# Seven block products for four more MLP tiles ahead of the attention loop, and three queries made inside the loop

## Chip, cores and metric

One core of one Trainium2 chip runs the whole kernel. The metric is the device time of one execution in microseconds. Five engines work side by side: the matrix engine (PE, with its weight loads listed as PEld), the vector engine (DVE), the activation engine (ACT), the general engine (POOL) and the engine that issues most transfers (SP). Matrix results go to PSUM banks, which DVE and ACT read.

## What is computed

The reference normalises x, runs attention of 32 heads over cached keys and values and an MLP mixer on the same normalised rows, and joins both with a gate:

```python
xn = _layernorm(x)                                   # 2048 x 512
# attention: q = xn @ wq, 32 heads of 128
scores = einsum("bhqd,bhkd->bhqk", q, k_cache) * 128 ** -0.5
s = softmax(scores) @ v_cache  ->  heads joined  @ wo
# MLP: D = 512, F = 1792
h = gelu(layernorm(xn) @ w1); hs = shifted(h) @ w2; x1 = xn + hs
g = silu(x1 + gelu(layernorm(x1) @ w3) @ w4)
return x + s * g
```

Inputs and output are bf16.

## The kernel before

**Tiles.** The 2048 rows are 16 tiles of 128 rows, four tiles make a chunk `c` of 512 rows.

**The MLP comes first.** `m1`, `m2` and `x1` make the first half of the MLP; `m3(c, f)` makes, for chunk `c`, a seventh of the 1792 hidden columns as 8 matmuls of 512 columns into a buffer `ps_s` (two buffers), and ACT's gelu writes it to `h2[c]`. The last product with `w4` is made in one of two ways:

- `pair_out(t)` takes tiles t and t+1 together and forms their product from seven block products, each 7 matmuls of 256 columns (49 in all), instead of 28 matmuls of 512. The block sums of the hidden rows come from `h_sums(t)`, four DVE instructions on 128x896 elements (L931). The results are put together by DVE additions (L948) while the products run, out of the banks `psX` (`xa` or `xm`, one buffer each, for `pa`) and `ps_o` (two buffers, for `pb` and `pc`). A second product is accumulated into `pb` and into `pc` after the first was read.
- A *held* tile is made as 14 matmuls of 512 columns, `m4`, that `held_mm(n)` spreads over the slots of the attention loop; when a tile is done, `held_out` adds it to `xall` (DVE), and two and four slots later the tanh (ACT) and the gate (DVE) follow.

Before the change tiles 0 to 7 go by pairs and tiles 8 to 15 are held. `gate_pair(t)` makes the gates of two tiles that went by pairs.

**The attention loop.** A unit is one head and one chunk of 512 query rows; there are 128 units, numbered in groups of 4 heads by 4 chunks, each of 8 slots (slot number n = 8u + p). In slot n, PE makes two score matmuls into `ps_s` (`s_slot`), ACT takes the exponential of both (L446), and PE makes two matmuls with the values for slot n - 10 (`pv_run`). DVE adds the exponentials of a unit (`add_first`, `add_half`, `add_next`, `fold`, `fold_last`) and, a unit later, sums, inverts and applies the row sums. Half of one addition goes to POOL in the units of `APART`. Every engine takes its instructions in the order in which the program writes them.

**Queries.** `q_ahead(u)` makes the query of a unit during the MLP: 4 matmuls into bank `xa` or `xm`, by turns of the list `made`, and a copy by ACT. Units 0 to 7, then 8 to 10, then 127 are made in this way. Units that are not in `made` and lie before unit 14 get theirs in the loop, two units ahead: one matmul in each of slots 3 to 6 into `xa` and a copy by DVE in slot 7 (`q_copy`). From unit 14 on two heads' queries come from seven block products; their block sums are `x_sum` (L366, on the normalised rows) and `w_sum` (L375, on `wq`).

**Output projection.** `wo_todo` is a queue of tiles whose four heads are finished. One tile takes slots 3 to 7 (`wo_mm` into `xm`, then a DVE copy or addition in `wo_post`). The first four tiles have to wait until `sacc` can be placed, which is where the MLP's buffers were (the pool `pS`, opened once the held tiles are done). Most later ones are made with seven block products as well, with sums `wo_sum` (on `wo`) and `o_sum`, added up by `wo_take` (L596). `CATCH` lists slots of unit 8 in which the waiting tiles are made, `PLAN` overrides the slots of single units.

Of the kernel before, what the change touches and what calls it, by code (L numbers as in the profile page):

```python
# [11 lines left out]
BF16 = mybir.dt.bfloat16  # L12
# [5 lines left out]
def kernel(  # L18
# [16 lines left out]
    P = nc.NUM_PARTITIONS  # L35
# [3 lines left out]
    Sq, D = x2d.shape  # L39
    _, H, Sk, Dh = A_k_cache.shape  # L40
# [3 lines left out]
    NT = Sq // P  # L44
# [3 lines left out]
    FC = F // P  # L48
    EPS = 1e-5
    SCALE = float(Dh) ** -0.5  # L50
    HG = 4
    NG = H // HG

    SPU = KC // 2
# [34 lines left out]
    qtp = ent(pool("qt", 6))  # L89
# [11 lines left out]
    pR = right.enter_context(pool("pR", side="right", reuse_waits="tile"))  # L101
# [21 lines left out]
    HEAD = 7  # L123
    XS = 3 * QT + 1
    TW = (2, 1, 0, 1)
# [3 lines left out]
    NU = len(units)  # L129
# [201 lines left out]
               xnT[:, dc, qt * 512:(qt + 1) * 512], dc == 0, dc == DC - 1)  # L331

    def q_copy(u, eng=None):
        pl, tag = (pR, "qR") if u < HEAD else (qtp, "qT")
        qT = pl.tile([P, 512], BF16, tag=tag, **(dict(bufs=HEAD) if u < HEAD else {}), name="qT")
        src, dst = st[u].pop("psq")[:], qT[:]
        if u in TURN:
            src = src.rearrange("d (r j) -> d j r", j=4)
            dst = dst.rearrange("d (j r) -> d j r", j=4)
        if eng is None:  # L340
            pin(nc.vector.tensor_copy(out=dst, in_=src))
        else:
            pin(nc.scalar.activation(out=dst, in_=src, func=ACT.Identity))
        st[u]["qT"] = qT[:]
# [208 lines left out]
    def wo_sum(g, i):  # L553
        w = wog[g]
        b11, b12, b21, b22 = (w[:, k, c] for k in (UP, DOWN) for c in (WL, WR))
        if i == 2 and g < NG - 2:
            out = b12
        else:
            j = 0 if i == 2 else i
            out = pS.tile([P, 2, D // 2], BF16, tag=f"tw{j}", bufs=TW[j], name="tw")[:]  # L560
        a, b = ((b12, b11), (b22, tw.get((g, 0))), (b22, b12), (b21, tw.get((g, 1))))[i]
        pin(nc.vector.tensor_tensor(out=out, in0=a, in1=b, op=ALU.subtract))
        tw[g, i] = out
# [267 lines left out]
    def q_ahead(u):  # L831
        q_mm(u, range(DC), ("xa", "xm")[len(made) % 2])
        q_copy(u, nc.scalar)
        made.append(u)
# [33 lines left out]
        x1(t, ps)  # L868
    for t in range(4):
        stats(xall[:, t, :], mv2, rs2, t)  # L870
    for u in range(2 * HG, 2 * HG + 3):
        q_ahead(u)
    banks = [(psO, "ps_o")] * 2 + [(psX, "xa"), (psX, "xm")]
    for t in range(4, 8):
        if t == 7:
# [95 lines left out]
    def gate_pair(t):  # L971
        th = [gate_tanh(t + i) for i in range(2)]
        for i in range(2):
            gate_silu(t + i, th[i])

    for c in range(2):
        h_sums(4 * c)
        h_sums(4 * c + 2)
        pair_out(4 * c, lambda: None)
        pair_out(4 * c + 2, lambda: gate_pair(4 * c))  # L980
        for f in range(FC // 2):
            m3(2 + c, f)
            if f == 1:
                gate_pair(4 * c + 2)
    left.close()
    pB = left.enter_context(pool("pB", reuse_waits="tile"))

# [16 lines left out]
            at((b - 4 - hh // 2) * SPU + (5, 7)[hh % 2], lambda h=h: load_wo(h))  # L1004

    heldps = {}
    held = deque((t, fc) for t in range(8, NT) for fc in range(FC))

    def held_out(t, n):
        x2(t, heldps.pop(t))  # L1010
# [2 lines left out]
        at(n + 4, lambda: gate_silu(t, th["a"]))  # L1013

    def held_mm(n):
        for _ in range((4, 10)[n] if n < 2 else 3 if n < SPU + 2 else 2 if n < 2 * SPU else 1 + (n % SPU in (1, 5, 7))):
            if not held:
                return
            t, fc = held.popleft()
            if fc == 0:  # L1020
                heldps[t] = psX.tile([P, 512], FP32, tag=("xa", "xm")[t % 2], name="ps_m")
            m4(t, heldps[t], (fc,))
            if fc == FC - 1:
                held_out(t, n)
# [28 lines left out]

    FIRST, LAST = 14, NU - 4
    BLOCK = [(g, qt) for g in range(NG - 1) for qt in range(QT)][1:-2]
    APART = range(2 * HG + 1, NU - 3)
    pairs = range(FIRST, LAST + 1, 2)
    q_plan = defaultdict(list)
    steps = defaultdict(list)
# [21 lines left out]
            which[u0 + n].append((o_sum, g, qt, i))  # L1081
    for g in range(NG - 1):
        u0 = ((g * QT + (g == 0)) * HG + 6) * SPU
        for i, n in ((0, -4), (2, -4 if 0 < g < NG - 2 else 4), (1, 4), (3, 12)):
            o_early[u0 + n].append((wo_sum, g, i))
    for i, (qt, u) in enumerate((qt, qt * HG + 5 + j) for qt in range(1, QT) for j in range(2)):
        at(u * SPU + 6, lambda qt=qt, i=i: sa_clear(qt, i % 2))
# [3 lines left out]
    for i, u in enumerate((10, 11, 12, 13, 14, 16, 18, 20)):  # L1091
# [2 lines left out]
        at(n - 2 * SPU + 4, lambda t=t, i=i: gate_load(t, i))  # L1094
        at(n + 3, lambda t=t: y_scale(t))
        at(n + 6, lambda t=t: y_add(t))
    CATCH = {2 * HG * SPU + p: x for p, x in {
        0: ((0, "xa"),), 1: ((1, "xa"),), 2: ((2, "xa"),), 3: ((0, "xm"),), 4: ((1, "xm"),),
        5: ((2, "xm"), (0, "xa")), 6: ((1, "xa"),), 7: ((2, "xa"),)}.items()}
    PLAN = {2 * HG: (), LATER + 6: (), LATER + 7: ((2, 0), (3, 1), (7, 2)), LATER + 8: ((1, 0), (3, 1), (4, 2), (6, 0), (7, 1)),  # L1100
            LATER + 9: ((0, 2), (2, 0), (3, 1), (7, 2))}

    def add_last(u):
# [13 lines left out]
        for fn, *args in plan.get(n, ()):  # L1117
            fn(*args)

    for j, u in enumerate((9, 9, 9, 9, 12, 12, 13, 13, 13, 16, 17, 17, 18, 19, 20, 20)):  # L1120
        at(u * SPU + 3, lambda qt=(j // 4 - 1) % QT, i=j % 4: x_sum(qt, i))
    for h in range(2, H, 2):
        for i, u in enumerate((((-4, -3, -3, -3), (-1, -1, 0, 0))[h % HG // 2] if h >= HG else (11,) * 4)):
            o_early[(h // HG * QT * HG + u) * SPU + 4].append((w_sum, h, i))

    for v in range(1, NU):
# [4 lines left out]
    for n in range(UB * SPU):  # L1131
# [29 lines left out]
            fold_last(u - 1)  # L1161
        if p == 3 and u - 1 in TURN:
            turn(u - 1)
        for part, tag in CATCH.get(n, ()):
            wo_slot(part, n, tag=tag)
        for v, k in ((u + 1, 3), (u + 2, 7)):
            if p == k and "psq" in st.get(v, ()) and (k == 3) == (v > FIRST):
                q_copy(v)
# [200 lines left out]
```

## Time and profile before

| | |
|---|---|
| median of 3 runs | 1223.53 us (1222.01 to 1224.49) |
| the profiled execution | 1222.83 us, its span 1221.1 us |
| PE busy | 1208.6 us, 99% |
| ACT busy | 1107.6 us, 91% |
| DVE busy | 1089.9 us, 89% |
| POOL busy | 297.6 us, 24% |

The span runs from the first to the last instruction; the profiled time holds 1.7 us more around it. Durations of matmuls overlap: the engine starts the next one before the listed end of the last, so the rate is read from starts. A row of a timeline gives start, duration, engine, line, operation, tiles, forms and count, and in brackets how long the engine was idle before it and what ended that.

### The profile page before, as it was taken

Reading aid. Unit: us, or ns where it says so; the run is one execution under the profiler, and the core shown is the slowest. Engines: PE = TensorE matmul, PEld = TensorE weight load, DVE = VectorE, ACT = ScalarE, POOL = GpSimd, SP = SyncE. Lnnn points to the kernel's source line nnn. Section 1 sums busy time; section 2 is a strip of 40 time slices with the busy share of each in tenths; the row PEclk is TensorE's granted clock in tenths of the full one; section 3 lists DMA queues with packets and bytes.
Section 4 is the critical chain, followed back from the end, with each engine's and each line's share of the span. In section 5 each row is a group of like instructions: output and inputs, shape, how many; then the busy total and the mean of one; then the engine's idle time right before and its main releaser. Section 6 shows DMA issues by size and latency. Waiting matters only on the chain.

```text
span 1221.1 us, 18821 instructions
## 1 busy us (share of the span) xinstructions
PE 1208.6 (99%) x6534; PEld 673.7 (55%) x6657; DVE 1089.9 (89%) x1931; ACT 1107.6 (91%) x1243; POOL 297.6 (24%) x221
## 2 busy tenths in 40 slices
PE   9999999999999999999999999999999999999998
PEld 6466444555555555555555555555555555555555
DVE  7863778999999999999999899999999999989997
ACT  6345999999999999999999999999999999999996
POOL 5300001233222222222222222222222222223320
PEclk9999999999999999999999999999999999999999
DMA  7662323434343434344344433444433534455552
GB/s 178 169 153 59 56 57 83 96 85 98 75 90 88 99 66 90 85 99 88 70 95 84 103 69 83 92 96 78 87 83 91 100 66 90 87 101 110 124 113 66
DMA packets 248159, 113.07 MB, mean 93 GB/s; under 512 B 195328, under 2 KB 231296, under 8 KB 248064
## 3 DMA queue, kind: packets, MB, share of 16 engines
q1 hardware_dynamic: 244560, 107.21, 40.9%
q0 software_dynamic: 2944, 4.20, 1.5%
q8 instruction: 52, 0.85, 0.3%
q14 instruction: 43, 0.35, 0.2%
q10 hardware_dynamic: 560, 0.46, 0.1%
HBM read 69.60 MB, written 4.45 MB: 61 GB/s over the span
## 4 chain that ended last, share of the span: by engine, by line
PE 92%; DVE 5%; issue 1%; DMA 1%; ACT 1%; SPq 0%; DVEq 0%; POOL 0%; ACTq 0%
PE ps_s L112 39%; PE ps_o L112 35%; PE ps_q L112 8%; PE ps_wo L112 8%; PE ps_m L112 3%; DVE acc L461 1%; DVE acc L452 1%; DVE sacc L596 1%; ACT pT L446 1%; DMA kT<-in_A_k_cache_dram 0%; DVE acc L457 0%; DVE sm L499 0%; DMA tT<-acc 0%; DMA xin<-in_A_x_dram 0%; PE ps_oh L112 0%
## 5 line engine op out<-in xcount | busy, mean ns | idle before, releaser
L446 ACT ACTIVATE pT<-ps_s 128x1024 bf16<-128x1024 f32 x1016 | 1016.6, 1028 | 44.5 <-PE ps_s L112 13.0
L112 PE MATMUL ps_s<-qT,kT 128*128 128x512 bf16 (+1 forms) x2056 | 607.5, 377 | 0.8 <-ACT pT L446 0.4
L112 PE MATMUL ps_o<-pT,vb 128*128 128x512 bf16 x1884 | 568.3, 379 | 4.7
L457 POOL TENSOR_TENSOR acc<-acc,pT 128x1024 bf16<-128x1024 bf16 x116 | 246.8, 2128 | 727.4 <-DVE acc L452 395.6
L112 PEld LDWEIGHTS <-vb 128*128 128x128 bf16 x1984 | 194.0, 98 | 216.5
L112 PEld LDWEIGHTS <-kT 128*128 128x128 bf16 x2064 | 231.0, 113 | 72.4 <-DVE qT L431 1.4
L461 DVE TENSOR_TENSOR acc<-acc,pT 128x2048 bf16<-128x2048 bf16 x138 | 168.9, 1224 | 21.5 <-ACT pT L446 5.5
L452 DVE TENSOR_TENSOR acc<-pT 128x2048 bf16<-128x2048 bf16 x127 | 154.7, 1218 | 11.2 <-ACT pT L446 11.1
L596 DVE TENSOR_TENSOR sacc<-ps_wo,sacc 128x512 f32<-128x512 f32 x200 | 121.6, 608 | 3.4 <-PE ps_wo L112 2.4
L523 DVE TENSOR_TENSOR oT<-ps_o,rb 128x512 bf16<-128x512 f32 x127 | 86.5, 681 | 6.6 <-DMA rb<-dr 5.9
L465 DVE TENSOR_TENSOR acc<-acc 128x1024 bf16<-128x1024 bf16 x127 | 87.3, 687 | 2.4
L499 DVE TENSOR_REDUCE sm<-tT 128x4 f32<-128x512 bf16 x124 | 83.9, 676 | 6.0 <-DMA tT<-acc 5.4
L457 DVE TENSOR_TENSOR acc<-acc,pT 128x1024 bf16<-128x1024 bf16 x116 | 79.6, 686 | 0.0
L112 PEld LDWEIGHTS <-wc 128*128 128x128 bf16 x448 | 43.8, 98 | 52.9
L112 PE MATMUL ps_wo<-wo_h,oT 128*128 128x256 bf16 (+1 forms) x294 | 70.7, 307 | 0.5
L112 PEld LDWEIGHTS <-oT 128*128 128x128 bf16 x428 | 41.6, 98 | 45.6
L112 PEld LDWEIGHTS <-so 128*128 128x128 bf16 x400 | 39.1, 98 | 48.4 <-issue 1.7
L112 PEld LDWEIGHTS <-wq_h 128*128 128x128 bf16 x396 | 38.7, 98 | 46.0
L112 PE MATMUL ps_q<-xnT,wq_h 128*128 128x256 bf16 (+1 forms) x281 | 58.2, 294 | 0.2
L301 ACT ACTIVATE h2T<-ps_s 128x1024 bf16<-128x1024 f32 x28 | 28.7, 1023 | 31.6 <-PE ps_s L112 31.6
L469 DVE TENSOR_TENSOR acc<-acc 128x512 bf16<-128x512 bf16 x127 | 53.4, 420 | 2.4
L112 PEld LDWEIGHTS <-w_sb 128*128 128x128 bf16 x368 | 33.5, 98 | 29.2
(134 smaller groups left out, 924.4 us busy)
## 6 DMA issues: line engine op xcount, KB each, us to landing
rb<-dr SPq DMA_DIRECT2D x127, 256.0 KB, 3.8
vb<-in_A_v_cache_dram SPq DMA_DIRECT2D x62, 256.0 KB, 3.0
wq_h<-in_A_wq_dram SPq DMA_DIRECT2D x32, 128.0 KB, 2.5
wo_h<-in_A_wo_dram SPq DMA_DIRECT2D x32, 128.0 KB, 2.3
w_sb<-in_B_w_dram SPq DMA_DIRECT2D x8, 256.0 KB, 4.6
kT<-in_A_k_cache_dram SPq DMA_TRANSPOSE x128, 2.6
gate<-xall POOLq DMA_DIRECT2D x16, 128.0 KB, 2.3
sacc<-in_A_x_dram POOLq DMA_DIRECT2D x8, 256.0 KB, 4.6
```

Of the source, the lines that this page charges most:

```text
L112: pin(nc.tensor.matmul(out=out, lhsT=lhsT, rhs=rhs, start=start, stop=stop, **kw))
L301: pin(nc.scalar.activation(out=h2[c][:, f], in_=ps[:], func=ACT.Gelu_apprx_tanh))
L446: pin(nc.scalar.activation(out=s["pT"][-1][:, jj:jj + 2, :], in_=sps[:], func=ACT.Exp, scale=SCALE))
L452: pin(nc.vector.tensor_tensor(out=s["acc"][:], in0=s["pT"][0][:], in1=s["pT"][1][:], op=ALU.add))
L457: pin(eng.tensor_tensor(out=a[:, part, :], in0=a[:, part, :], in1=e[:, part, :], op=ALU.add))
L461: pin(nc.vector.tensor_tensor(out=a[:], in0=a[:], in1=st[u]["pT"][i][:], op=ALU.add))
L465: pin(nc.vector.tensor_tensor(out=a[:, 0:2, :], in0=a[:, 0:2, :], in1=a[:, 2:4, :], op=ALU.add))
L469: pin(nc.vector.tensor_tensor(out=a[:, 0, :], in0=a[:, 0, :], in1=a[:, 1, :], op=ALU.add))
L499: pin(nc.vector.tensor_reduce(out=sm[:], in_=s["tT"][:], axis=mybir.AxisListType.X, op=ALU.add))
L523: pin(nc.vector.tensor_tensor(out=to, in0=o, in1=rb, op=ALU.mult))
L596: pin(nc.vector.tensor_tensor(out=out, in0=ps, in1=out, op=ALU.add))
```

## The change

- Tiles 8 to 11 are made by pairs in the MLP, ahead of `m3(3)`, so that tiles 4 to 11 run as four pairs in a row; `h_sums(8)` stands between pairs 4 and 6, `h_sums(10)` between pairs 6 and 8. The gates of tiles 6 to 11 fall into `m3(3)`.
- Only tiles 12 to 15 are held, and `held_mm` spreads their 56 matmuls over slots 0 to 55: 4, 6, two each in slots 2 to 8, one each in 9 to 15, then five a unit.
- The queries of units 8 to 10 are no longer made in the MLP but in units 6 to 8. Unit 127's query gets a pool entry of its own (`qL`).
- The first four tiles of the output projection go one in unit 7, two in unit 8 (the first of them in slots 0 to 2, bank `xa`), one in unit 9.
- Block sums of `x` move from units 9 to 16 to units 8 to 13, the first sums of `wq` from unit 11 to units 8 and 9; one block of `wo` sums of the last such group moves to the `qT` pool; `APART` starts at unit 7 instead of 9.

```diff
     def q_copy(u, eng=None):
-        pl, tag = (pR, "qR") if u < HEAD else (qtp, "qT")
-        qT = pl.tile([P, 512], BF16, tag=tag, **(dict(bufs=HEAD) if u < HEAD else {}), name="qT")
+        pl, tag, n = (pR, "qR", HEAD) if u < HEAD else (qtp, "qT", 5) if u < NU - 1 else (qtp, "qL", 1)
+        qT = pl.tile([P, 512], BF16, tag=tag, bufs=n, name="qT")
...
         if i == 2 and g < NG - 2:
             out = b12
+        elif i == 2:
+            out = qtp.tile([P, 2, D // 2], BF16, tag="qT", bufs=5, name="tw")[:]
         else:
-            j = 0 if i == 2 else i
-            out = pS.tile([P, 2, D // 2], BF16, tag=f"tw{j}", bufs=TW[j], name="tw")[:]
+            out = pS.tile([P, 2, D // 2], BF16, tag=f"tw{i}", bufs=TW[i], name="tw")[:]
...
-    for u in range(2 * HG, 2 * HG + 3):
-        q_ahead(u)
     banks = [(psO, "ps_o")] * 2 + [(psX, "xa"), (psX, "xm")]
     for t in range(4, 8):
         if t == 7:
             q_ahead(NU - 1)
         x1(t, m2(t, *banks[t % 4 if t < 7 else 0]))
...
-    for c in range(2):
-        h_sums(4 * c)
-        h_sums(4 * c + 2)
-        pair_out(4 * c, lambda: None)
-        pair_out(4 * c + 2, lambda: gate_pair(4 * c))
-        for f in range(FC // 2):
-            m3(2 + c, f)
-            if f == 1:
-                gate_pair(4 * c + 2)
+    h_sums(0)
+    h_sums(2)
+    pair_out(0, lambda: None)
+    pair_out(2, lambda: gate_pair(0))
+    for f in range(FC // 2):
+        m3(2, f)
+        if f == 1:
+            gate_pair(2)
+    h_sums(4)
+    h_sums(6)
+    pair_out(4, lambda: None)
+    h_sums(8)
+    pair_out(6, lambda: gate_pair(4))
+    h_sums(10)
+    pair_out(8, lambda: None)
+    pair_out(10, lambda: None)
+    for f in range(FC // 2):
+        m3(3, f)
+        if f in (0, 2, 4):
+            gate_pair(6 + f)
...
-    held = deque((t, fc) for t in range(8, NT) for fc in range(FC))
+    held = deque((t, fc) for t in range(3 * HG, NT) for fc in range(FC))
...
     def held_mm(n):
-        for _ in range((4, 10)[n] if n < 2 else 3 if n < SPU + 2 else 2 if n < 2 * SPU else 1 + (n % SPU in (1, 5, 7))):
+        for _ in range((4, 6)[n] if n < 2 else 2 if n < SPU + 1 else n < 2 * SPU or n % SPU in (0, 2, 4, 5, 7)):
...
-    APART = range(2 * HG + 1, NU - 3)
+    APART = range(2 * HG - 1, NU - 3)
...
-        for i, n in ((0, -4), (2, -4 if 0 < g < NG - 2 else 4), (1, 4), (3, 12)):
+        for i, n in ((0, -4), (2, -4 if g else 4), (1, 4), (3, 12)):
             o_early[u0 + n].append((wo_sum, g, i))
...
-    CATCH = {2 * HG * SPU + p: x for p, x in {
-        0: ((0, "xa"),), 1: ((1, "xa"),), 2: ((2, "xa"),), 3: ((0, "xm"),), 4: ((1, "xm"),),
-        5: ((2, "xm"), (0, "xa")), 6: ((1, "xa"),), 7: ((2, "xa"),)}.items()}
-    PLAN = {2 * HG: (), LATER + 6: (), LATER + 7: ((2, 0), (3, 1), (7, 2)), LATER + 8: ((1, 0), (3, 1), (4, 2), (6, 0), (7, 1)),
+    CATCH = range(2 * HG * SPU, 2 * HG * SPU + 3)
+    PLAN = {LATER + 6: (), LATER + 7: ((2, 0), (3, 1), (7, 2)), LATER + 8: ((1, 0), (3, 1), (4, 2), (6, 0), (7, 1)),
...
-    for j, u in enumerate((9, 9, 9, 9, 12, 12, 13, 13, 13, 16, 17, 17, 18, 19, 20, 20)):
+    for j, u in enumerate((8, 8, 8, 9, 9, 9, 9, 11, 11, 13, 17, 17, 18, 19, 20, 20)):
         at(u * SPU + 3, lambda qt=(j // 4 - 1) % QT, i=j % 4: x_sum(qt, i))
     for h in range(2, H, 2):
-        for i, u in enumerate((((-4, -3, -3, -3), (-1, -1, 0, 0))[h % HG // 2] if h >= HG else (11,) * 4)):
+        for i, u in enumerate((((-4, -3, -3, -3), (-1, -1, 0, 0))[h % HG // 2] if h >= HG else (8, 8, 9, 9))):
...
-        for part, tag in CATCH.get(n, ()):
-            wo_slot(part, n, tag=tag)
+        if n in CATCH:
+            wo_slot(p, n, tag="xa")
```

## The prediction

> **What bounds the kernel now.** I read the page first, then the list of waits of the matrix engine, then the timelines of the stretches that the diff touches.
>
> ```profile
> span 1221.1 us, 18821 instructions
> ...
> PE 1208.6 (99%) x6534; PEld 673.7 (55%) x6657; DVE 1089.9 (89%) x1931; ACT 1107.6 (91%) x1243; POOL 297.6 (24%) x221
> ```
>
> The matrix engine (PE) is busy 99% of the span. Its waits, summed over the run, are next to nothing:
>
> ```profile
> PE ps_wo L112 <- DVE sacc L596: 0.5, 1, 0.5
> PE ps_s L112 <- ACT pT L446: 0.4, 1, 0.4
> ```
>
> So the time is the sum of PE's work, and whatever makes PE wait anywhere is added to it in full. The change is to be priced as PE work removed, PE waits added, PE waits removed. The rates come from the end of the MLP (pair of tiles 6 and 7, then `m3(3)`, then the first units):
>
> ```profile
> 97.83 0.93 PE L112 MATMUL ps_m<-w_sb,h2T 128*128 128x256 bf16 x7
> ...
> 103.18 12.25 PE L112 MATMUL ps_s<-xn2T,w_sb 128*128 128x512 bf16 x54
> 115.27 0.59 PE L112 MATMUL ps_s<-qT,kT 128*128 128x512 bf16 x2
> ...
> 116.57 0.59 PE L112 MATMUL ps_s<-qT,kT 128*128 128x512 bf16 x2
> ...
> 119.16 0.59 PE L112 MATMUL ps_s<-qT,kT 128*128 128x512 bf16 x2
> ```
>
> A pair takes 49 matmuls of 256 columns, 103.18 - 97.83 = 5.35 us, 0.109 each and 0.764 for a product of seven. `m3(3)` issues 56 of 512 columns (the record misses two) in 115.27 - 103.18 = 12.09 us, 0.216 each.
>
> **Work.** Tiles 8 to 11 as held tiles were 56 x 0.216 = 12.09 us; as two pairs they are 10.70. The saving is **1.40 us** (1.3 to 1.5). The 12 query matmuls (2.59 us) only move from the MLP into units 6 to 8.
>
> The Trainium skill (TensorE: Matmul & The Clock Gate, section Back-to-back issue gap) gives about 131 ns a matmul at 512 columns and 81 ns at 128 for a sustained stream with its weight loads. By it, an estimate, a pair costs at least 49 x 81 = 3.97 us against 28 x 131 = 3.67, a loss of 0.3 or more. The trace disagrees: 0.216 and 0.109, so narrow products lose nothing here.
>
> **Wait 1: the last query made early.** `q_ahead` alternates between the banks `xa` and `xm` by the number already made. Without units 8 to 10 that number is 8, not 11, when unit 127 is made, so its bank is `xa` instead of `xm`. `m2(6)`, issued just ahead of it, also writes `xa`, and PE must wait until `x1(6)` on DVE has read it.
>
> ```profile
> 30.85 2.75 PE L112 MATMUL ps_o<-w_sb,hT 128*128 128x512 bf16 x12
> 33.44 1.03 PE L112 MATMUL ps_q<-xnT,wq_e 128*128 128x512 bf16 x4
> ```
> ```profile
> 29.91 0.18 DVE L210 BATCH_NORM_AGGREGATE mv<-bn 128x2 f32<-128x6 f32 x1
> 31.92 0.69 DVE L283 TENSOR_TENSOR xall<-ps_o,xall 128x512 bf16<-128x512 f32 x1 [1.82 <-PE ps_o L112]
> ...
> 208.36 0.68 DVE L655 COPY sacc<-ps_wo 128x512 f32<-128x512 f32 x1
> 208.96 0.68 DVE L523 TENSOR_TENSOR oT<-ps_o,rb 128x512 bf16<-128x512 f32 x1
> ```
>
> With the queries gone PE wants the bank at 33.44 - 2.59 = 30.85. DVE still has statistics until 30.09; then `x1(4)`, `x1(5)`, `x1(6)` follow from 30.0, 0.60 apart (instructions of this size at 208.36 and 208.96 in the loop), and the third ends at 31.2 + 0.69 = 31.9. PE waits **1.1 us** (0.9 to 1.2, as the two DVE ends may be 0.1 off each; not below, since no other work of PE's stands ahead of that query in program order). Behind it PE has `m2(7)` and the last `m1`; all later MLP work moves 1.5 us earlier and keeps its order.
>
> **Wait 2: sums between the pairs.** `h_sums(8)` and `h_sums(10)` stand on DVE behind pairs 4 and 6, whereas the earlier sums ran under `m3`.
>
> ```profile
> 86.84 0.62 DVE L931 TENSOR_TENSOR hs<-h2T 128x896 bf16<-128x896 bf16 x1
> ...
> 89.10 0.62 DVE L931 TENSOR_TENSOR hs<-h2T 128x896 bf16<-128x896 bf16 x1
> ...
> 97.62 0.84 DVE L948 TENSOR_TENSOR xall<-ps_o,mt 128x256 bf16<-128x256 f32 x2
> 99.98 0.43 DVE L948 TENSOR_TENSOR mt<-ps_m,mt 128x256 f32<-128x256 f32 x1 [1.52 <-ACT mt L954]
> 100.51 0.42 DVE L948 TENSOR_TENSOR mu<-ps_o,mt 128x256 f32<-128x256 f32 x1
> ...
> 101.50 0.42 DVE L948 TENSOR_TENSOR xall<-ps_o,mu 128x256 bf16<-128x256 f32 x1
> ...
> 102.97 1.28 DVE L318 SCALAR_TENSOR_TENSOR xall<-th,xall 128x512 bf16<-128x512 bf16 x2
> 104.17 0.75 DVE L948 TENSOR_TENSOR xall<-ps_o,mt 128x256 bf16<-128x256 f32 x2
> ```
>
> Four sums take 89.10 - 86.84 = 2.26 us and DVE idles only 1.52 between pairs. On the clock of these rows: the sums run 98.38 to 100.64, so pair 6's additions start 0.66 late, and PE's later products in that pair wait about 0.2 for their banks to be read; pair 8 starts on PE at 103.40. Its third product needs `ps_o` back, which the 104.17 rows, now 0.66 late, free at 105.3: 0.4 us. DVE then does `h_sums(10)`, 105.50 to 107.76, and pair 8's first addition starts there. The product into the same bank as that pair's third needs the second addition's result (0.53 + 0.42 later, 108.76, wanted at 107.6), and the last one the fourth's (1.52 + 0.42 later, 109.75). PE ends pair 8 at 110.52, where 97.83 + 2 x 5.35 = 108.53 was due. That is **2.0 us** (1.0 to 2.7: the nearest cover is the 1.52 of idle; the upper end is DVE's full lag behind an undelayed pair 8). Pair 10 has no sums behind it and waits no more. No gain is possible here, as no addition gets earlier.
>
> **Wait 3: the first ten slots.** PE may be two slots ahead of the exponentials, as `ps_s` has two buffers.
>
> ```profile
> 115.47 1.02 ACT L301 ACTIVATE h2T<-ps_s 128x1024 bf16<-128x1024 f32 x1 [0.70 <-PE ps_s L112]
> 116.51 1.28 ACT L446 ACT_TABLE_LOAD   x1
> 117.81 4.08 ACT L446 ACTIVATE pT<-ps_s 128x1024 bf16<-128x1024 f32 x4
> 121.79 0.62 ACT L314 ACTIVATE th<-xall 128x512 bf16<-128x512 bf16 x1
> 122.31 4.98 ACT L446 ACTIVATE pT<-ps_s 128x1024 bf16<-128x1024 f32 x5
> ```
>
> The first exponential ends at 117.81 + 1.02 = 118.83. Slot 2's scores come 14 matmuls after slot 0's instead of 18, at 118.30, and wait 0.6 for it. Exponentials in a row take about (4.08 - 1.02) / 3 = 1.0, down to 0.90 when they queue, and a tanh 0.52 (121.79 to 122.31). Slots 2 to 8 now hold four matmuls, 0.863, slot 9 three, 0.647: six slots at 0.04 more make 0.25, the tanh of tile 12 in slot 5 costs 0.6 at slot 8, slot 9 another 0.25. Sum **1.7 us** (1.0 if the 0.04s vanish and the tanh costs half; 1.9 if the queue never reaches 0.90). From slot 10 on five matmuls (1.08) exceed 0.90 again. Tanhs of later held tiles fall between slots of four matmuls: **0.25** (0 to 0.5, the 0.6 above being undamped). The gates of tiles 6 to 11, now in `m3(3)`, cost nothing: ACT idles 0.70 per chunk there, and two tanhs come every second chunk.
>
> **Wait 4: unit 8.** The caught-up `wo` tile of slots 0 to 2 sits in `xa`; DVE copies it at slot 2, and the query of unit 10 wants `xa` at slot 3. Ahead of that copy DVE has the same run as in unit 9 of before, plus two clears. Behind that query on PE stand the scores of the rest of unit 8, and behind those ACT.
>
> ```profile
> 207.75 0.69 DVE L341 CAST qT<-ps_q 128x512 bf16<-128x512 f32 x1 [1.14 <-PE ps_q L112]
> ...
> 213.48 0.75 DVE L571 TENSOR_TENSOR so<-oT 128x512 bf16<-128x512 bf16 x2
> ```
> ```profile
> 194.99 0.27 DVE L545 MEMSET sacc<- 128x256 f32 x1
> 195.18 0.63 DVE L655 COPY sacc<-ps_wo 128x512 f32<-128x512 f32 x1
> ```
> ```profile
> 207.77 0.59 PE L112 MATMUL ps_s<-qT,kT 128*128 128x512 bf16 x2
> ```
>
> The run starts with the last slot's scores (207.75 beside 207.77) and takes 213.48 - 207.75 = 5.73; clears 2 x 0.19, copy 0.63: read at 6.74. PE wants the bank after 4 + 6 + 6 + 4 + 4 = 24 matmuls, 5.18. **1.6 us** (0.9 to 2.0: without the half addition that now goes to POOL, and with one more copy queued).
>
> **Waits removed.** DVE is behind in units 12 to 16, and PE waits three times there:
>
> ```profile
> 232.72 0.59 PE L112 MATMUL ps_o<-pT,vb 128*128 128x512 bf16 x2
> 233.78 0.38 PE L112 MATMUL ps_wo<-wo_h,so 128*128 128x256 bf16 x2 [0.47 <-DVE sacc L596]
> ...
> 242.43 0.38 PE L112 MATMUL ps_wo<-tw,oT 128*128 128x256 bf16 x2
> 243.25 0.62 PE L112 MATMUL ps_s<-qT,kT 128*128 128x512 bf16 x2 [0.44 <-ACT pT L446]
> ...
> 267.72 0.59 PE L112 MATMUL ps_o<-pT,vb 128*128 128x512 bf16 x2
> 268.43 0.38 PE L112 MATMUL ps_wo<-wo_h,so 128*128 128x256 bf16 x2
> ```
> ```profile
> 230.92 0.42 DVE L366 TENSOR_TENSOR xs<-xnT 128x512 bf16<-128x512 bf16 x1
> ```
>
> From the due start (two matmuls after the row above) to the start they are 233.78 - 233.15 = 0.63, 243.25 - 242.65 = 0.60 and 268.43 - 268.15 = 0.28. Two sums like the one at 230.92 leave unit 12, two unit 13, one unit 16, at 0.34 to 0.42 each. Against that, unit 9 gains a query copy and two `wq` sums: by the spacings above an estimate of 9.1 us on DVE beside 40 x 0.216 = 8.6 on PE, so 0.45 late. I take back **1.35** of 1.5 (0.2, if the lateness stays, to 1.5).
>
> **Costed at nothing.** Units 7 and 8 give half an addition to POOL, busy 24%; no queue of DMAs is reordered, SP's and POOL's only get the gates of tiles 8 to 11 earlier; the `wo` block that moves to the `qT` pool has a buffer free since unit 8.
>
> **Sum.** -1.40 + 1.1 + 2.0 + 1.7 + 0.25 + 1.6 - 1.35 = **+3.9 us**. The profiled execution took 1222.83, 0.70 under the median 1223.53; on the median the forecast is **1227.4**. All lower ends give +0.8 (1224.3), all upper ends +6.8 (1230.3). A measurement of this kernel can tell about 0.2%, 2.45 us, from no change.
>
> **Rivals.** (a) *DVE keeps pace.* If its sums and copies slip in before PE asks, waits 1, 2 and 4 (4.7) vanish: -0.8, 1222.7. For it: the two waits found now are small. Against: 2.26 does not fit in 1.52, and 5.73 is a measured run. It decides once the run ahead of the unit 8 copy is under 4.5. Chance 0.14. (b) *Only the pairs' wait is absent* (1.9, 1225.4, no clear difference): 0.10. (c) *Both ACT and DVE keep up*: wait 3 goes too, -2.5, 1221.0; 0.05. (d) *The lag in units 9 to 16 stays*, so nothing is taken back: +5.2, 1228.7; 0.13. Moving sums to units 8 and 9, with three query copies more, speaks for it. (e) *Half as wide costs more than half*: at 0.15 a matmul instead of 0.109 the 98 would add 4.0, 1231.4. The four pairs in the trace speak against; 0.01. The Trainium skill (same page and section) would have this sign.
>
> The forecast has 0.57. Slower by over 0.2% is forecast, (d) and (e), 0.71; no difference (a) and (b), 0.24; faster (c), 0.05. The range 1224.3 to 1230.3 leaves out (a), (c) and (e), 0.20.
>
> **What would show it.** In the list of PE's waits: one of about 1 us for `ps_q<-xnT,wq_e` near 31, waits of `ps_o` and `ps_m` on DVE L948 in the third of the four pairs, `ps_s` waiting on `pT` in the first ten slots, one `ps_q` on DVE L655 in unit 8, and none near units 13 and 14. `m3(3)` should start at 103.18 - 2.59 + 1.1 + 10.7 + 2.0 = 114.4. If PE shows no wait in the pairs or in unit 8, the prediction is wrong at DVE's order; if a longer wait stands elsewhere, I missed it.

## The result and the profile after

The changed kernel takes **1227.99 us** (median of 6 runs, 1227.65 to 1228.5), the kernel before 1223.22 on the same chip (6 runs, 1222.01 to 1224.49): ratio **1.0039, 95% interval 1.0026 to 1.0052**, 4.8 us slower. The forecast was +3.9 us and 1227.4. The profiled execution of the changed kernel took 1228.15 us with a span of 1226.4; against the profiled execution of before that is +5.3.

First the page of the changed kernel: the span, and the busy time of each engine.

```profile
span 1226.4 us, 18938 instructions
...
PE 1208.2 (99%) x6577; PEld 677.6 (55%) x6699; DVE 1099.0 (90%) x1956; ACT 1104.3 (90%) x1242; POOL 301.4 (25%) x223
```

The busy time of PE does not show the change: it has 43 more recorded matmuls and 0.4 us less to do by this row, because the listed ends are modelled and overlap. The list of what PE waited for does show it (total, times, longest):

```profile
PE ps_q L112 <- DVE sacc L656: 1.5, 1, 1.5
PE ps_s L112 <- ACT pT L446: 1.5, 3, 0.7
PE ps_m L112 <- DVE mt L947: 1.2, 1, 1.2
PE ps_wo L112 <- DVE sacc L597: 1.1, 1, 1.1
PE ps_q L112 <- DVE xall L283: 1.1, 1, 1.1
...
PE ps_o L112 <- DVE xall L947: 0.2, 1, 0.2
```

Both lists also hold waits in the first 10 us (1.0 for the warm-up's first matmul, the same in both); leaving these aside, the two longest were 0.5 and 0.4 before. Each line shown is one of the forecast's waits, except the fourth, which was not foreseen; of the three waits in the second line the longest belongs to the later tanhs. The list counts idle time only. PE's true loss is longer by about 0.16 each time, as a matmul's listed end lies that far behind the due start of the next; so each wait below is measured from the start that was due (0.216 us a matmul of 512 columns, 0.109 of 256) to the start. The matmuls themselves, from the timeline of PE:

```profile
28.18 2.75 PE L112 MATMUL ps_o<-w_sb,hT 128*128 128x512 bf16 x11
32.02 1.02 PE L112 MATMUL ps_q<-xnT,wq_e 128*128 128x512 bf16 x4 [1.09 <-DVE xall L283]
...
96.41 0.93 PE L112 MATMUL ps_m<-w_sb,h2T 128*128 128x256 bf16 x7
...
101.97 0.93 PE L112 MATMUL ps_m<-w_sb,h2T 128*128 128x256 bf16 x7
102.74 0.93 PE L112 MATMUL ps_m<-w4t,hs 128*128 128x256 bf16 x7
103.86 1.69 PE L112 MATMUL ps_o<-w4t,hs 128*128 128x256 bf16 x14 [0.20 <-DVE xall L947]
106.79 0.92 PE L112 MATMUL ps_m<-w_sb,h2T 128*128 128x256 bf16 x7 [1.24 <-DVE mt L947]
...
109.08 0.93 PE L112 MATMUL ps_m<-w_sb,h2T 128*128 128x256 bf16 x7
...
114.42 12.25 PE L112 MATMUL ps_s<-xn2T,w_sb 128*128 128x512 bf16 x54
...
130.12 0.59 PE L112 MATMUL ps_s<-qT,kT 128*128 128x512 bf16 x2 [0.43 <-ACT pT L446]
...
136.13 0.59 PE L112 MATMUL ps_s<-qT,kT 128*128 128x512 bf16 x2 [0.40 <-ACT pT L446]
...
165.16 0.38 PE L112 MATMUL ps_m<-w_sb,h2T 128*128 128x512 bf16 x1
166.24 0.59 PE L112 MATMUL ps_s<-qT,kT 128*128 128x512 bf16 x2 [0.70 <-ACT pT L446]
...
198.78 0.59 PE L112 MATMUL ps_o<-pT,vb 128*128 128x512 bf16 x2
200.92 0.38 PE L112 MATMUL ps_q<-xnT,wq_h 128*128 128x512 bf16 x1 [1.54 <-DVE sacc L656]
...
981.36 0.59 PE L112 MATMUL ps_o<-pT,vb 128*128 128x512 bf16 x2
983.04 0.38 PE L112 MATMUL ps_wo<-wo_h,so 128*128 128x256 bf16 x2 [1.09 <-DVE sacc L597]
```

Pairs 6, 8 and 10 start at 96.41, 101.97 and 109.08, and `m3(3)` at 114.42. Pair 10 waits for nothing and takes 5.34 us for its 49 matmuls, 0.109 each. Pair 6 takes 5.56 and pair 8 takes 7.11, beside the 5.35 of a pair before.

| term of the sum | forecast | in the trace | how |
|---|---|---|---|
| Work | -1.40 | -1.4 | two pairs at 5.34 against 56 x 0.216 = 12.09 |
| Wait 1, last early query | +1.1 | +1.25 | 32.02 - (28.18 + 12 x 0.216) |
| Wait 2, sums between the pairs | +2.0 | +1.97 | (5.56 - 5.35) + (7.11 - 5.35) |
| Wait 3, first ten slots | +1.7 | +1.75 | 0.59 at 130.12, 0.56 at 136.13, 0.27 at 137.96, six of 0.055 |
| later tanhs | +0.25 | +0.86 | 166.24 - (165.16 + 0.216) |
| Wait 4, query of unit 10 | +1.6 | +1.70 | 200.92 - (198.78 + 2 x 0.216) |
| Waits removed | -1.35 | -1.5 | none of the three is left |
| sum up to unit 18 | +3.9 | +4.6 | the trace: first exponential of unit 18 at 282.62, before at 277.98 |
| wait of L597 at 983 | none | +1.25 | 983.04 - (981.36 + 2 x 0.216) |

From unit 18 to the end the kernel loses another 0.7: the wait at 983 less what before had lost in small waits over the same stretch. The first exponential of the loop starts 11.24 us later than before (129.05, was 117.81), since the work of held tiles has moved ahead of it; by the first of unit 8 only +3.9 is left. Unit 8 adds 2.3, of which 1.70 is its wait, and by unit 18 the waits that are gone have brought the sum to +4.6.

### The profile page after: what moved, and what is told of

The parts are those of the page before. It is cut to its first block, busy times and chain, and to the rows that moved or that the text cites. A ratio compares the mean times of both kernels' runs of the same rounds, so it can differ in the third digit from the quotient of the medians.

```text
span 1226.4 us, 18938 instructions
## 1 busy us (share of the span) xinstructions
PE 1208.2 (99%) x6577; PEld 677.6 (55%) x6699; DVE 1099.0 (90%) x1956; ACT 1104.3 (90%) x1242; POOL 301.4 (25%) x223
## 4 chain that ended last, share of the span: by engine, by line
PE 91%; DVE 4%; ACT 2%; issue 1%; DMA 1%; POOL 0%; DVEq 0%; SPq 0%; ACTq 0%
PE ps_s L112 39%; PE ps_o L112 35%; PE ps_q L112 8%; PE ps_wo L112 8%; ACT pT L446 2%; PE ps_m L112 1%; DVE acc L461 1%; DMA rb<-dr 0%; DVE hs L930 0%; DVE oT L523 0%; DVE sm L499 0%; DMA xin<-in_A_x_dram 0%; PE ps_oh L112 0%; DVE mt L947 0%; DMA dr<-rc 0%
## 5 line engine op out<-in xcount | busy, mean ns | idle before, releaser
L457 POOL TENSOR_TENSOR acc<-acc,pT 128x1024 bf16<-128x1024 bf16 x118 | 250.9, 2126 | 732.6 <-DVE acc L452 379.8
L461 DVE TENSOR_TENSOR acc<-acc,pT 128x2048 bf16<-128x2048 bf16 x136 | 166.4, 1224 | 21.8 <-ACT pT L446 5.3
L597 DVE TENSOR_TENSOR sacc<-ps_wo,sacc 128x512 f32<-128x512 f32 x200 | 121.8, 609 | 4.2 <-PE ps_wo L112 2.8
```

Of the source, the lines that this page charges most:

```text
L457: pin(eng.tensor_tensor(out=a[:, part, :], in0=a[:, part, :], in1=e[:, part, :], op=ALU.add))
L461: pin(nc.vector.tensor_tensor(out=a[:], in0=a[:], in1=st[u]["pT"][i][:], op=ALU.add))
L597: pin(nc.vector.tensor_tensor(out=out, in0=ps, in1=out, op=ALU.add))
```

## The experiments

Three theories stood against each other. **A**: PE is the bound everywhere, so each wait is on the path and adds in full; take it away and PE's later work is earlier by just that. **B**: slack or lateness elsewhere takes it up, and the time stays. **F**, on the waits late in the loop: the fetch of a block of PE's instructions makes the data transfers late that are under way at that moment.

They ran on three chips, each with its own runs of before: bank, unit 10's query, sums and slots beside 1225.22 us; the repeat, `xa` in before, the warm-up and all mends beside 1223.38; tanh, block sums and the last one beside 1224.98. Ratios are to the before of the same chip. The chips differ: the median broadcast of `rb` (the inverse row sums, 256 KB, 127 in a run) lands after 3.8 to 3.9 us on the second, where before is the fastest of the three, and after 4.0 to 4.1 on the other two. One wait is about 0.1% of the time, as much as an interval is wide to one side, and the changed kernel itself was run again on the second chip only; so the verdicts on single waits rest on the places and shifts in the traces, and the ratios are only a check.

**The changed kernel again.**

> The changed kernel itself, beside the next three on one chip. Both theories: 1.0039 times the kernel before (4.8 us more), with the same five waits of PE at the same places, the one near 983 us too if it belongs to the program and not to chance.

1228.1 us, ratio 1.0041 (1.0027 to 1.0054). All waits of the table come back at their places: 0.36 and 1.40 in the pairs, 0.59, 0.56 and 0.27 in the first slots, 0.86, 1.71 in unit 8, 0.98 near 983. Wait 1 varies most: 1.89 us here, 0.95 to 1.46 in the six other traces of kernels with the same code there. In this run a load of x landed later: the DVE statistics that wait for it start at 14.54, in the profile of the changed kernel at 13.56, and DVE carries that 0.97 along to `x1(6)`.

**The last early query in the other bank.** Undoes the turn of the banks alone.

```diff
-        q_mm(u, range(DC), ("xa", "xm")[len(made) % 2])
+        q_mm(u, range(DC), "xm" if u == NU - 1 else ("xa", "xm")[len(made) % 2])
```

> The changed kernel, with the query of unit 127 put back into bank xm. Theory A (every wait of PE is on the path and adds in full): the wait of ps_q<-xnT,wq_e on DVE L283 near 31 us (1.25 us from due start to start) is gone, m3(3) starts at 114.42 - 1.25 = 113.2, the time is 1227.99 - 1.25 = 1226.7. Theory B (work behind a wait is late anyway, so the time comes back as another wait): the wait is gone, m3(3) starts later than 113.9 or a wait of about the same size stands behind it, and the time stays within 0.5 of 1228.0.

1228.82 us, ratio 1.0025 (1.0015 to 1.0036). PE's timeline at this place:

```profile
29.71 1.46 PE L112 MATMUL ps_o<-w_sb,hT 128*128 128x512 bf16 x6
31.27 1.02 PE L112 MATMUL ps_q<-xnT,wq_e 128*128 128x512 bf16 x4
```

The query starts at 31.27, 0.26 after it was due, now for the landing of `xnT`. The wait for L283 is gone, and everything from `m3(0)` up to unit 12 is 0.75 earlier than in the changed kernel: A. Of the 1.25, the 0.26 is lost again because the transposes are the next thing late, and 0.24 because this run reached the place that much later.

**The same bank in the kernel before.** The one cost alone, added instead of taken away.

```diff
-        q_mm(u, range(DC), ("xa", "xm")[len(made) % 2])
+        q_mm(u, range(DC), "xa" if u == NU - 1 else ("xa", "xm")[len(made) % 2])
```

> The kernel before, with one wait of the change put in: the query of unit 127 made in bank xa instead of xm. Theory A (every wait of PE is on the path): PE wants the bank at 33.44 and x1(6) reads it until 33.64 + 0.69 = 34.33, so the query starts 0.95 later, m3(0) starts 0.95 later (46.5), and the time rises by 0.95. Theory B (slack further on takes it up): the first score matmul and the end move by less than 0.3.

1224.53 us, ratio 1.0010 (1.0001 to 1.0019). The row of the query:

```profile
34.37 1.02 PE L112 MATMUL ps_q<-xnT,wq_e 128*128 128x512 bf16 x4 [0.78 <-DVE xall L283]
```

The wait is 0.95 from the due start, and the later work up to unit 12 is 0.92 to 0.93 later than in before, without a loss or a gain on the way through the rest of the MLP and twelve units: A, where it is cleanest. From unit 14 on the two traces part by other waits of 0.4 to 0.7, and by the last units this run is 2.3 later: in this trace nothing takes the wait up.

**The sums of the pairs.** Pairs 8 and 10, with their sums, go behind the fourth chunk of `m3(3)`.

```diff
     pair_out(4, lambda: None)
-    h_sums(8)
     pair_out(6, lambda: gate_pair(4))
+    h_sums(8)
     h_sums(10)
-    pair_out(8, lambda: None)
-    pair_out(10, lambda: None)
     for f in range(FC // 2):
+        if f == 4:
+            pair_out(8, lambda: None)
+            pair_out(10, lambda: gate_pair(8))
         m3(3, f)
-        if f in (0, 2, 4):
+        if f in (0, 4):
             gate_pair(6 + f)
```

> The changed kernel, with pairs 8 and 10 moved behind the fourth chunk of m3(3), so that h_sums(8) and h_sums(10) run on DVE under m3(3) as the earlier sums do; the gates of tiles 8 to 11 go to pair 10 and the fifth chunk. Theory A: PE has no wait on L947 in any pair; the two waits (0.36 + 1.40) and the product's late start go, the first score matmul comes 1.8 us earlier, time 1227.99 - 1.8 = 1226.2. Theory B (the pairs' additions themselves are what PE waits for): a wait on L947 of 0.5 or more is left in pairs 8 and 10, time 1227 or more.

1227.14 us, ratio 1.0017 (1.0008 to 1.0027). No wait on L947 is left in the list, and the loop starts 1.73 earlier than in the changed kernel although `m3(0)` started 0.23 later in this run: 1.96, the whole of wait 2. A: with the 32 matmuls of four chunks (6.9 us) to lie beside, the eight sums cost nothing.

**More held matmuls in the first slots.** Ten in slot 1 and three each in slots 2 to 8, as before the change, and fewer later.

```diff
-        for _ in range((4, 6)[n] if n < 2 else 2 if n < SPU + 1 else n < 2 * SPU or n % SPU in (0, 2, 4, 5, 7)):
+        for _ in range((4, 10)[n] if n < 2 else 3 if n < 9 else 2 if n < 10 else n < 2 * SPU or (n % SPU in (1, 3, 6) and n < 47) or n == 55):
```

> The changed kernel, with the held matmuls in slots as 4, 10, three each in slots 2 to 8, two in 9, one each in 10 to 15, then three a unit and the last in slot 55. Theory A (PE waits for exponentials where a slot holds less than 0.9 us of matmuls): the waits of ps_s on pT in the first ten slots (0.59, 0.56, 0.27 and six of 0.04) shrink to 0.1, the later ones near 166 (0.86) change with where tiles end, by reckoning 0.3 in place of it; time 1227.99 - 1.7 to 2.2 = 1225.8 to 1226.3. Theory B (ACT's total work in units 0 to 6 is the bound): the same waits come back in units 2 to 5, time 1227.5 or more.

1227.64 us, ratio 1.0018 (1.0009 to 1.0028). The four long waits on exponentials are gone, and one of 0.39 stands at 148.96, where the changed kernel has none. The first exponential of unit 8 is 1.63 earlier than in the changed kernel, 1.98 when the 0.35 by which this run started later is set aside. Wait 3 and the tanh had made 1.75 + 0.86 = 2.61; less the 0.39 that is 2.2, so A holds but for 0.2, which sits in waits too small to be named.

**Unit 10's query two slots later.** Two matmuls each in slots 5 and 6 of unit 8.

```diff
-(v - 2) * SPU + dc + 3
+(v - 2) * SPU + (5 + dc // 2 if v == 2 * HG + 2 else dc + 3)
```

> The changed kernel, with the four query matmuls of unit 10 in slots 5 and 6 of unit 8 (two each) instead of one in each of slots 3 to 6; the matrix work is the same. Theory A: bank xa is read 2.6 us before it is wanted again, the wait on DVE L656 (1.70 us) is gone, the first exponential of unit 9 comes 1.7 earlier, time 1227.99 - 1.7 = 1226.3. Theory B (DVE is the bound around unit 8): the lateness of DVE moves on, the waits near units 13, 14 and 16 of the kernel before return (0.63, 0.60, 0.28 there), time 1227.5 to 1228.

1227.8 us, ratio 1.0019 (1.0009 to 1.0029). The query in unit 8, from the timeline of PE:

```profile
201.08 0.59 PE L112 MATMUL ps_o<-pT,vb 128*128 128x512 bf16 x2
201.51 0.59 PE L112 MATMUL ps_q<-xnT,wq_h 128*128 128x512 bf16 x2
201.94 0.38 PE L112 MATMUL ps_wo<-wo_h,oT 128*128 128x512 bf16 x1
```

It follows without a gap. Unit 9 starts 1.56 earlier although unit 8 started 0.14 later: 1.70, the whole wait. The waits near units 13, 14 and 16, which B expected back, do not come. In this run's profile the gain is lost again later, by waits of 0.61, 0.61 and 0.32 at 322.7, 467 and 586; the one at 983 is here 0.71. They need not come from this edit: three other runs, without it, have a wait at one of these places (0.54 at 322.9 with the sums moved, 0.68 at 584.9 with more held matmuls, 0.56 at 586.1 with the later tanh), all on the two chips with the slower broadcasts, and the changed kernel and its repeat have none there. In this run each follows a transfer that DVE waited for 7 to 10 us ahead (`rb` twice, once `tT`, the sums that DVE reduces). That speaks for late transfers and against B; which of them F explains was not taken apart.

**The tanh of held tiles two slots later.**

```diff
-        at(n + 2, lambda: th.update(a=gate_tanh(t)))
-        at(n + 4, lambda: gate_silu(t, th["a"]))
+        at(n + 4, lambda: th.update(a=gate_tanh(t)))
+        at(n + 6, lambda: gate_silu(t, th["a"]))
```

> The changed kernel with the tanh and the gate of each held tile two slots later. Theory A (every wait of the matrix engine adds in full): the wait of 0.86 us near 166, behind a tanh that itself waits 0.58 for the addition of tile 14, is gone or under 0.2, the exponentials from the fifth unit on start 0.7 to 0.9 earlier than in the changed kernel, all earlier waits stay, and the ratio to the kernel before goes from 1.0040 to about 1.0033. Theory B (slack elsewhere takes it up): the later tanh makes its own wait two slots on, or later waits grow by as much, and the ratio stays at 1.0040. The two ratios are closer than the interval, so the place of the waits decides.

1228.37 us, ratio 1.0028 (1.0017 to 1.0038). ACT's timeline there, first of the changed kernel, then of this one:

```profile
161.05 3.02 ACT L446 ACTIVATE pT<-ps_s 128x1024 bf16<-128x1024 f32 x3
164.64 0.63 ACT L314 ACTIVATE th<-xall 128x512 bf16<-128x512 bf16 x1 [0.58 <-DVE xall L310]
165.18 2.83 ACT L446 ACTIVATE pT<-ps_s 128x1024 bf16<-128x1024 f32 x3
```

```profile
159.43 6.84 ACT L446 ACTIVATE pT<-ps_s 128x1024 bf16<-128x1024 f32 x7
166.16 0.63 ACT L314 ACTIVATE th<-xall 128x512 bf16<-128x512 bf16 x1
166.68 1.94 ACT L446 ACTIVATE pT<-ps_s 128x1024 bf16<-128x1024 f32 x2
```

In the changed kernel the tanh holds ACT idle for 0.58 behind a DVE addition, and the exponentials queue behind it. Two slots later it waits for nothing, the wait of 0.86 is gone, and unit 8 starts 0.66 earlier after allowing for the start 0.11 later: A for the most part. Of the 0.2 not recovered, 0.17 is a shorter wait at 167.76. The earlier waits did not all stay as expected: the tanh of tile 12 moved too, and 0.56 and 0.27 became one of 0.78 at 138.07.

**The moved block sums alone.** The kernel before with the two lists of the change.

```diff
-    for j, u in enumerate((9, 9, 9, 9, 12, 12, 13, 13, 13, 16, 17, 17, 18, 19, 20, 20)):
+    for j, u in enumerate((8, 8, 8, 9, 9, 9, 9, 11, 11, 13, 17, 17, 18, 19, 20, 20)):
...
-        for i, u in enumerate((((-4, -3, -3, -3), (-1, -1, 0, 0))[h % HG // 2] if h >= HG else (11,) * 4)):
+        for i, u in enumerate((((-4, -3, -3, -3), (-1, -1, 0, 0))[h % HG // 2] if h >= HG else (8, 8, 9, 9))):
```

> The kernel before with only the lists of block sums of x and of wq taken from the change (units 8 to 13 for x, 8 and 9 for the first of wq). Theory A: the three waits of 0.63, 0.60 and 0.28 us at 233.8, 243.3 and 268.4 go and nothing new comes in units 8 to 11: 1.5 us less, ratio 0.9988, the exponential of the eighteenth unit 1.3 to 1.5 earlier. Rival (the lateness of the vector engine only moves): waits of 0.5 to 1.5 us come up in units 8 to 11 instead, where unit 8 of this kernel still makes all its waiting output tiles, and the ratio is 0.9995 to 1.0005.

1223.32 us, ratio 0.9986 (0.9977 to 0.9995). PE's timeline in units 12 to 15:

```profile
232.82 0.59 PE L112 MATMUL ps_o<-pT,vb 128*128 128x512 bf16 x2
233.69 0.38 PE L112 MATMUL ps_wo<-wo_h,so 128*128 128x256 bf16 x2 [0.27 <-DVE sacc L596]
...
242.34 0.38 PE L112 MATMUL ps_wo<-tw,oT 128*128 128x256 bf16 x2
242.56 0.59 PE L112 MATMUL ps_s<-qT,kT 128*128 128x512 bf16 x2
...
259.21 0.38 PE L112 MATMUL ps_wo<-tw,oT 128*128 128x256 bf16 x2
259.90 0.62 PE L112 MATMUL ps_s<-qT,kT 128*128 128x512 bf16 x2 [0.31 <-DVE qT L431]
```

The expected picture holds in part. The wait at 243 and that at 268 are gone (0.60 and 0.28); that at 233.8 falls from 0.63 to 0.44; a new one of 0.47 stands at 259.90, on a query copy. No wait comes up in units 8 to 11, so the rival fails. Up to unit 18 the trace gains 0.62 of the 1.5. The lists alone do not give the whole of **Waits removed**; in the changed kernel, with the output tiles, the half additions and the queries moved as well, all of it goes. Which of these does the rest was not taken apart. The ratio's interval (0.6 to 2.8 us) takes in both sizes.

**The warm-up in half as many instructions.** PE makes 46 matmuls of 128 columns at the start; this kernel makes 23 of 256, the same columns with 46 instructions fewer (matmuls and weight loads). Nothing later is changed, but each block of PE's code is fetched at another place of the program.

```diff
-    warm = const.tile([P, P], BF16, name="warm")
+    warm = const.tile([P, 2 * P], BF16, name="warm")
...
-            mm(wps[:, 0:P], warm[:], warm[:], True, True)
+            mm(wps[:, 0:2 * P], warm[:, 0:P], warm[:], True, True)
...
-    warm_mm(44)
+    warm_mm(22)
...
-    warm_mm(2)
+    warm_mm(1)
```

> The changed kernel, with 23 warm-up matmuls of 256 columns instead of 46 of 128, so that PE has 46 instructions fewer ahead of everything and the same busy time. In the transfers' record a 16 KB packet of instructions falls into the flight of each late row-sum broadcast (all 8 of over 4.6 us in the kernel before). Theory F (a fetch of PE's code delays the transfers in flight, and DVE and PE wait for them): fetches come 46 of 256 instructions later, about 4 us in the loop, the one at 972.7 falls clear of the broadcast of unit 99 (968.8 to 974.5), that broadcast lands in 3.9, the wait of ps_wo on DVE L597 near 983 (1.25) is below 0.4; other broadcasts become late instead. Rival (the place in the data or chance): that wait stays at 0.8 or more.

1227.62 us, ratio 1.0036 (1.0022 to 1.0050). DVE's timeline ahead of the place of the wait at 983, first of the changed kernel, then of this one:

```profile
971.98 0.68 DVE L431 TENSOR_TENSOR qT<-ps_q,tq 128x512 bf16<-128x512 f32 x1
974.57 0.69 DVE L523 TENSOR_TENSOR oT<-ps_o,rb 128x512 bf16<-128x512 f32 x1 [1.91 <-DMA rb<-dr]
```

```profile
971.90 0.68 DVE L431 TENSOR_TENSOR qT<-ps_q,tq 128x512 bf16<-128x512 f32 x1
972.77 0.69 DVE L523 TENSOR_TENSOR oT<-ps_o,rb 128x512 bf16<-128x512 f32 x1 [0.19 <-DMA rb<-dr]
```

And the DMA view of the stretch in which that broadcast was under way, the queues with packets, bytes and share, then the broadcast's time to landing; first of the changed kernel, then of this one:

```profile
q1 hardware_dynamic: 883, 0.44, 93.7%
q8 instruction: 1, 0.02, 1.0%
...
rb<-dr SPq DMA_DIRECT2D x1, 256.0 KB, 5.7
```

```profile
q1 hardware_dynamic: 1052, 0.50, 54.6%
...
rb<-dr SPq DMA_DIRECT2D x1, 256.0 KB, 3.8
```

With an instruction packet in the stretch the broadcast takes 5.7 us, without it 3.8. The record of the single packets shows the delay itself: in the changed kernel 28 of the small data packets that start between 972.32 and 972.88 are held until 974.42 to 974.46, for 1.6 to 2.1 us, around the instruction packet (972.70 to 973.65); here no packet of that stretch takes over 0.2. DVE loses 1.91 for it, gets through its queue late, and PE pays eight microseconds later. Here PE has no wait of L597 above 0.1 at all. Three other broadcasts are late instead, as expected (5.0 to 5.2 us, at 293, 858 and 951), but none of them costs PE a wait of over 0.1. F.

**All mends together.** The five edits above on the changed kernel: bank, sums, slots, unit 10's query, tanh.

> The changed kernel with all mends: query of unit 127 in xm, unit 10's query matmuls in slots 5 and 6 of unit 8, pairs 8 and 10 behind the fourth chunk of m3(3), held matmuls as 4, 10, 3 (slots 2 to 8), 2, then 1, then three a unit, and the tanh of a held tile two slots later. Theory A (waits add up, so mends do too): 4.8 - 1.25 - 1.7 - 1.8 - 2.2 = -2.2 against the kernel before, ratio 0.998, and only late transfers are left among PE's waits after 100 us. Theory B (DVE or ACT is the bound behind the waits): the mends overlap, ratio 1.000 or more.

1221.09 us (11 runs, 1220.62 to 1221.75), ratio **0.9981 (0.9972 to 0.9990)**: the change is now faster than before. Behind the first microseconds PE has four waits of over 0.25 left, 0.27 at 31.4, 0.33 at 147.8, 0.48 at 975.5 and 0.30 at 1009.9 from the due starts. In its list:

```profile
PE ps_wo L112 <- DVE sacc L597: 0.3, 1, 0.3
PE ps_s L112 <- ACT pT L446: 0.2, 1, 0.2
```

By A the mends take 1.0 + 1.97 + 1.75 + 0.86 + 1.70 = 7.3 off, less the 0.33 that is left in the slots; from +4.8 that gives -2.2, and -2.3 was measured.

**All mends and the shorter warm-up.**

> The version with all five mends, and its 46 warm-up matmuls of 128 columns made as 23 of 256, so that the matrix engine has 46 instructions fewer ahead of all the rest and fetches its code at other places. Theory F (a fetch of code that falls on a transfer makes it late, and the matrix engine pays): the waits of 0.48 us near 975 and of 0.30 near 1010 are gone or at other places, and if none replaces them the ratio to the kernel before goes from 0.9981 to about 0.9975. Rival (these two waits come from the order of the work): they stand where they were and the ratio is 0.998.

1222.06 us beside 1224.98, ratio **0.9976 (0.9967 to 0.9985)**, the lowest ratio of all runs. The waits at 975 and 1010 are gone, and one of 0.46 stands at 393. That the code's place moves these waits is what F expects; the step from 0.9981 to 0.9976 is inside the intervals and shows nothing by itself.

## Why the prediction was right

The sign and the place of every forecast wait hold, except for one step inside wait 2, and all sizes but one hold to within 0.2. Between the medians 4.8 us were found for 3.9; between the profiled executions 5.3, 1.4 more than forecast: 0.6 of it is one mis-sized term, 0.1 the other terms together, and 0.7 the waits late in the loop, which were not in the sum. The time alone would not tell the forecast (1227.4) from rival (d) (1228.7); the places of the waits do.

**What bounds the kernel.** Right, and the base of all: a wait added in before (0.95) and five waits taken from the changed kernel moved the following stretch of PE by their own length, to within 0.2 where nothing else was late next.

**Work.** Right: 0.109 and 0.216 hold in two more pairs. Rival (e) is out. The figures of the Trainium skill for a sustained stream (TensorE: Matmul & The Clock Gate, section Back-to-back issue gap) do not describe this kernel; the same section has a formula for a single matmul, N / 2.4 + 2.5 ns, which gives 216 and 109, and it says that in a stream this over-counts for wide matmuls and under-counts for narrow ones. Here the stream runs at it for both.

**Wait 1.** Right in place and cause; 1.25 here and 0.95 to 1.89 in other runs, a wider spread than the 0.9 to 1.2 given. The bounds took DVE's times as exact to 0.1, and they hang on when x lands.

**Wait 2.** The sum is right (1.97 for 2.0), the third product's 0.4 too (0.36), and `m3(3)` starts at 114.42 for 114.4. But the step that should have cost most was the wrong one. The prediction let PE wait in the pair's last products, which accumulate behind additions two and four. The trace has the wait at the fifth product (106.79, `ps_m`): `pair_out` puts it into `pa` again, the bank that the *first* addition reads:

```profile
105.78 0.62 DVE L930 TENSOR_TENSOR hs<-h2T,hs 128x896 bf16<-128x896 bf16 x1
106.32 0.41 DVE L947 TENSOR_TENSOR mt<-ps_m,mt 128x256 f32<-128x256 f32 x1
106.84 0.42 DVE L947 TENSOR_TENSOR mu<-ps_o,mt 128x256 f32<-128x256 f32 x1
```

That addition ends at 106.73, PE goes on at 106.79, and after that the later products are late enough to find their banks read. The working skipped this product, although the signs to look for name `ps_m`. DVE's queue itself was forecast right: on this run's clock, 1.42 earlier, the first addition was due at 106.34 and starts at 106.32, and the bank of the last product was due at 108.33 and is read at 108.25. Let go at 106.79, PE gets to that product at 108.31. So the skipped step and the one in the working bind within 0.1 of each other, and it is luck of this order of work that the sum came out right.

**Wait 3.** Right in each piece: 0.59 at slot 2 (0.6), 0.56 at slot 8 (0.6), 0.27 at slot 10 (0.25), and 0.055 instead of 0.04 in six slots.

**Later tanhs.** The mis-sized term: 0.86 for 0.25, above its upper end of 0.5. The prediction took them as lying between slots of four matmuls, at a tanh's own length of 0.52, damped. It did not look at when the tanh's input is ready. The list of `held_mm` now ends tile 14 at the start of a unit, where DVE's queue holds the last sums of exponentials of the unit before ahead of the addition (L310):

```profile
161.63 1.19 DVE L461 TENSOR_TENSOR acc<-acc,pT 128x2048 bf16<-128x2048 bf16 x1
...
163.92 0.68 DVE L310 TENSOR_TENSOR xall<-ps_m,xall 128x512 bf16<-128x512 f32 x1
```

The tile's last matmul starts at 161.28, the addition only at 163.92. The tanh waits for it in ACT's queue, and the exponentials behind the tanh with it. The range for an undamped tanh was 0.6 from a case without that wait.

**Wait 4.** Right: 1.70 for 1.6, at the query and behind the copy that were named.

**Waits removed.** Right for the changed kernel (-1.5 for -1.35), but the reason given was too narrow: the moved block sums alone give 0.62 in the trace, and waits of 0.44 and 0.47 are left there. The lag that rival (d) expects in units 9 to 16 is absent in the changed kernel: between 201 and 983 PE has no wait there of over 0.15.

**What was not in the sum.** The wait at 983. Nothing in the prediction looked at how transfers fall against the fetches of code. The edit adds 43 recorded matmuls and their weight loads ahead of this place, so the fetches move in the program. In before the longest wait behind unit 18 was 0.40, at 868.

**The rivals.** (a), (b) and (c) are out: DVE and ACT were late where the rows said so. Of these, (a) had been bounded by a measured run of DVE instructions (5.73 us against the 5.18 that PE needs to get there), and that was the better guide than PE's short list of waits before.

## What to carry to other kernels

Where one engine is at 99%, price a change by walking each bank and buffer it touches: when the engine asks for it, and when the last reader's queue gets there, with everything that stands ahead of that reader. An edit that saves matrix work can lose more than that through the order of the other engines' queues; here -1.4 - 1.5 of gain was buried under 7.5 of waits, and five edits of a line or a few each, which issue the same work in another order, turned +0.39% into -0.19%. For an operation that moves, ask for its input's queue as well as its own.

## What the runs showed of the hardware

PE's code comes in packets on a queue of its own kind, and a packet can delay the data that is under way. In the trace of the changed kernel the queue q8 carries 52 of them:

```profile
q8 instruction: 52, 0.85, 0.3%
```

That is 16 KB each, one about every 24 us. Spread over PE's 6577 matmuls and 6699 weight loads it is 64 bytes an instruction, so it reads as PE's code. In before 45 of the 127 broadcasts of `rb` had an instruction packet in flight, of q8 or of a second such queue, q14; they take 4.09 us in the mean and the others 3.66, so most packets do little and a few do 2 us. All 9 broadcasts of over 4.6 us are among the 45 (the expectation of the warm-up run counts 8), in the changed kernel 5 of 6, and over all 13 traces 116 of 129, where about a third of all broadcasts have a packet in flight.

A hold like the one at 972 (in the loop, a dozen or more data packets of up to 4 KB kept for over 1.4 us and let go together) is found 28 times in the 13 traces. Each of the 28 has a packet of q8 in it and ends 0.77 to 0.89 us behind that packet's end; some begin up to 0.6 before it starts, so it is not the packet's bytes alone that hold the data up.

The Trainium skill (Runtime: NRT & Kernel Launch, section Instruction fetch mechanics) describes such a refill, in 16 KiB blocks of 256 instructions, and calls its cost mostly hidden. The block size agrees with these rows. On PE's own issue no cost shows; on the transfer in flight it does, and as the transfer's reader is an engine 90% busy, PE paid 1.25 us for it at 983. Shifting the code by 46 instructions removed the wait at 983 in the changed kernel and moved those of the mended one. What in the DMA engines holds the transfer up was not taken apart.
